# Attention and two dense blocks on one core: the first keys loaded in two parts with the constants behind them, and the end of each attention half reordered

## The chip, the cores and the metric

The kernel runs on one core of a Trainium2 chip. The metric is the device time of one execution in microseconds (us), read as the median of several executions. The core has five engines, each of which runs its own instructions in the order in which they stand: PE (matrix multiplication), DVE (vector), ACT (tables of functions, here tanh and exp), POOL and SP (the last issues most of the transfers). Transfers run on 16 DMA engines that all queues share.

## The reference

Three stages follow one another. All of it is float32, and the kernel keeps that accuracy on PE by splitting each operand into a high and a low part and adding three products.

```python
def _attn_ref(q, k, v, cap):          # 4 x 12 heads, 448 positions, 64 wide
    scale = 1.0 / np.sqrt(q.shape[-1])
    scores = scale * np.matmul(q, k.transpose(0, 1, 3, 2))
    scores = cap * np.tanh(scores / cap)
    scores = scores - np.max(scores, axis=-1, keepdims=True)
    attn = np.exp(scores)
    attn = attn / (np.sum(attn, axis=-1, keepdims=True) + 1e-09)
    return np.matmul(attn, v)
...
def _moe_ref(x, w_in, w_out):         # 1792 tokens, 768 -> 2048 -> 768
    h = x @ w_in
    return (h - np.tanh(h)) @ w_out
...
def _moe2_ref(x, w_in, w_out, g_ln):  # 768 -> 1024 -> 768
    h = x @ w_in
    sm = softmax(h)                   # over the row, with 1e-09 in the sum
    solu = h * sm
    ln = (solu - mean(solu)) / sqrt(var(solu) + 1e-06) * g_ln
    return ln @ w_out
```

## The kernel before, in words

The batch is cut into two halves, and each half runs attention, the first block and the second block in turn. Attention of a half takes 12 pairs of heads; a pair fills the 128 partitions (two heads of 64). The loop of `attention` runs over i from -4 to 13 and starts the steps of several pairs in each turn: `load` and `load_v` fetch q with the keys (tile kq, 512 columns of keys, then 448 of q) and v (vf), `split_qk` makes the high part kqh (L250) and the low part kql (L252) on DVE, `scores` does the score matmuls on PE (L274, L276) and tanh on ACT (L278), exp follows on ACT (L288), `values` multiplies with v on PE (L308) and carries the row sums of exp along as row 64 of its result, and `evict` (L318) copies that result and its sums into ou. Three small transfers then spread the sums over partitions for a cheap reciprocal: rs<-ou, `finish1` (reciprocal L327, rd<-rs at L329, and ou<-ou at L330, which brings the second head of the pair to partitions 64 to 127), and `finish2` (rb<-rd at L336, a broadcast of the reciprocals to all partitions). `finish3` multiplies (L355) and splits the result into xh (L356) and xl (L357), the operands of the first block.

The last pair, 11, goes another way: `finish_last` takes two reciprocals of one row of 448 (L345) and spreads each with a matmul over the selector sel (L346).

The first block's up projection on PE (hp, L403 and L405) begins with the pairs that are done, goes round its weights, and needs xh and xl of the pairs 8 to 11 last. Its nonlinear part on DVE (first instruction L437) and ACT follows each hp.

In the first half the weights arrive as 64-bit words (tile st, L101), are narrowed on DVE (L106 to L108, tile f), cast on ACT (L114) and their low part taken on DVE (L115; L168 for those that `early` spreads over attention as fetch, `high` and `low`). They are written to DRAM (d<-w, L131) so that the second half only reloads them (L186). Thirteen of these writes wait until the end of the first half's attention and stand together there in SP's queue (`while pending`).

The order on every engine inside attention is that of the code. The constants of the cap (capt and what is worked out of it: tscale, ncap, shift, guard, gcol; L75 to L86) stand at the start of the program.

Of the kernel before, what the change touches and what calls it, by code (L numbers as in the profile page):

```python
# [29 lines left out]
def fused_kernel(ctx, tc, qk_in, v, cap, w1, w2, w3, w4, gln, out):  # L30
# [15 lines left out]
    KW = qk_in.shape[3] - S  # L46

# [27 lines left out]
    nc.vector.reciprocal(tscale, capt)  # L75
    nc.vector.tensor_scalar_mul(tscale, tscale, 1.0 / math.sqrt(D))
    ncap = const.tile([P, 1], F32, name="ncap")
    nc.vector.scalar_tensor_tensor(ncap, capt, -1.0, capt, ALU.mult, ALU.min)
    shift = const.tile([P, 1], F32, name="shift")
    nc.vector.tensor_scalar(shift, ncap, 64.0, 0.0, ALU.add, ALU.min)  # L80
    guard = const.tile([P, 1], F32, name="guard")
    nc.vector.scalar_tensor_tensor(guard, ncap, math.log(1e-9), shift, ALU.add, ALU.add)
    nc.scalar.activation(guard, guard, AF.Exp)
    gcol = const.tile([P, 1], F32, name="gcol")
    nc.vector.memset(gcol, 0.0)
    nc.vector.tensor_copy(gcol[D:D + 1], guard[D:D + 1])  # L86
# [49 lines left out]
    def early():  # L136

        units = [(f"1_{c}_{half}_{i}", w1u[(c * 2 + half) * (NK // 2) + i])
                 for c in range(2) for half in range(2) for i in range(NK // 2)]
        units += [(f"2_0_{d}", w2u[d]) for d in range(NK)]  # L140
        units = units[:WA]
        stage = {}

        def fetch(k):
            key, src = units[k]
            if key in saved:
                w = wp.tile([P, 2, 512], F32R, tag="w", name="w")
                nc.gpsimd.dma_start(w.bitcast(F32), saved[key].bitcast(F32))
                ahead[key] = w
            else:  # L150
                stage[k] = words(src, nc.gpsimd)

        def high(k):
            key = units[k][0]
            if k in stage:
                w = wp.tile([P, 2, 512], F32R, tag="w", name="w")
                ahead[key] = w
                stage["f", k] = narrowed(stage.pop(k))

        def mid(k):  # L160
            if ("f", k) in stage:
                nc.scalar.copy(ahead[units[k][0]][:, 0], stage["f", k])

        def low(k):
            if ("f", k) in stage:
                key = units[k][0]
                w = ahead[key]
                nc.vector.tensor_tensor(w[:, 1], stage.pop(("f", k)), w[:, 0].bitcast(F32), ALU.subtract)  # L168
                pending.append((key, w))

        return fetch, high, mid, low
# [52 lines left out]
    def attention(ap, hb, xh, xl):  # L224
# [9 lines left out]
        def load(p):  # L234
            bb, j = pairs[p]
            kq = ap.tile([P, KW + S], F32, tag="kq", name="kq", bufs=3)
            with tc.high_priority(offset=400 if hb == 0 and p == 0 else 0):
                (nc.sync if hb == 0 and p < 3 else nc.gpsimd).dma_start(kq, qk_in[HB * hb + bb, j])
            raw[p] = kq

        def load_v(p):
            bb, j = pairs[p]
            vf = ap.tile([P, 8, VW], F32, tag="vf", name="vf", bufs=3)
            nc.gpsimd.dma_start(vf, v[HB * hb + bb, j])
            vs[p] = (vf,)

        def split_qk(p):
            kq = raw.pop(p)
            h = ap.tile([P, KW + S], F32R, tag="kqh", name="kqh")
            nc.vector.tensor_copy(h, kq)  # L250
            l = ap.tile([P, KW + S], F32R, tag="kql", name="kql")
            nc.vector.tensor_tensor(l, kq, h.bitcast(F32), ALU.subtract)  # L252
            qk[p] = (h, l)

# [8 lines left out]
        def score(p, r):  # L263
# [5 lines left out]
            cs = slice(P * r, P * (r + 1))  # L269
# [69 lines left out]
        def finish_last(p):  # L339

            ou, _ = fin[p]
            rec = ap.tile([P, 7, S], F32, tag="t", name="rec")
            rb = pst("rbp", "o")[:, 0, :S]
            for hh in range(2):
                nc.vector.reciprocal(rec[D:D + 1, hh], ou[D:D + 1, hh])  # L345
                nc.tensor.matmul(rb, sel[D:D + 1, hh], rec[D:D + 1, hh], start=(hh == 0), stop=(hh == 1))  # L346
            nc.sync.dma_start(ou[D:, 0], ou[:D, 1])
            fin[p] = (ou, rb)
# [14 lines left out]
        for i in range(-4, n + 2):  # L363
# [3 lines left out]
            at(i - 1, evict)  # L367
            if i == n:
                finish_last(n - 1)
            at(i - 2, finish2, m=n - 1)  # L370
# [12 lines left out]
            at(e - 3, low, m=WA)  # L383
            at(e - 1, high, m=WA)
            at(i - 4, finish3)
        finish3(n - 2)
        finish3(n - 1)
        while pending:
# [282 lines left out]
```

## Time and profile before

| | |
|---|---|
| median of 3 runs | 961.9 us (960.1, 961.9, 963.87) |
| the profiled execution | 963.42 us, its span 961.1 us |
| mean granted clock of TensorE in it | 0.996 |
| PE busy | 935.8 us (97%) |
| DVE, ACT, POOL busy | 612.0 us (64%), 420.6 us (44%), 50.1 us (5%) |
| moved by DMA | 145.65 MB, mean 152 GB/s |

A busy share is an average over stages. PE, at 97%, leaves some 25 us in which it does nothing, and the busy time also holds the stretch in which its clock was granted at half. The times below are counted from the start of the span.

### The profile page before, as it was taken

What the parts mean: (1) busy time and instruction counts of PE and PEld (TensorE: products, weight loads), DVE (VectorE), ACT (ScalarE), POOL (GpSimd) and SP (SyncE); (2) the same over time, 40 slices, a digit from 0 to 9 for tenths busy, and PEclk for the clock granted to TensorE, in tenths of its full rate; (3) what the DMA queues carried; (4) which work ended last, traced back from release to release, by engine and by line L of the source; (5) the groups of instructions that cost most, each with busy time, mean ns of one, the idle gap of its engine ahead of it and who ended that gap; (6) DMA issues with size and microseconds to landing.
All of it is one profiled execution on the core that took longest, in us unless ns stands there. A gap on an engine that the chain in (4) does not pass through costs nothing.

```text
span 961.1 us, 11645 instructions
## 1 busy us (share of the span) xinstructions
PE 935.8 (97%) x4512; PEld 751.5 (78%) x4512; DVE 612.0 (64%) x946; ACT 420.6 (44%) x502; POOL 50.1 (5%) x91
## 2 busy tenths in 40 slices
PE   6999989999998999999989999999999999999998
PEld 3444569998998898888855555799999999988887
DVE  4677777989989895588335665596064553405751
ACT  6878508645436122352147775085250331211321
POOL 2221000000000000001011110000000000000000
PEclk9999989999999999999999999999999999999999
DMA  6565483188585874442135642243232232312311
GB/s 243 175 173 163 129 314 138 52 295 310 201 296 188 294 267 172 158 171 89 50 140 181 198 155 72 94 150 107 91 121 107 102 110 88 110 41 91 127 50 49
DMA packets 48946, 145.65 MB, mean 152 GB/s; under 512 B 11708, under 2 KB 16188, under 8 KB 48892
## 3 DMA queue, kind: packets, MB, share of 16 engines
q1 hardware_dynamic: 41404, 114.57, 34.5%
q0 software_dynamic: 7344, 30.35, 9.8%
q8 instruction: 35, 0.57, 0.3%
q14 instruction: 19, 0.16, 0.1%
q10 hardware_dynamic: 144, 0.00, 0.0%
HBM read 98.73 MB, written 43.33 MB: 148 GB/s over the span
## 4 chain that ended last, share of the span: by engine, by line
PE 73%; DVE 15%; DMA 8%; ACT 2%; issue 2%; SPq 0%; DVEq 0%; ACTq 0%
PE hp L403 11%; PE o L308 10%; PE op L459 8%; PE hp L405 5%; PE s L274 5%; PE op L461 4%; PE hp L222 4%; PE hp L221 4%; PE hp L220 4%; PE oab L556 3%; PE oab L560 3%; PE oab L557 3%; DMA st<-in_moe_w_out_dram 2%; DVE f L107 2%; DVE f L108 2%; DMA st<-in_moe_w_in_dram 2%
## 5 line engine op out<-in xcount | busy, mean ns | idle before, releaser
L403 PE MATMUL hp<-xh,w 128*128 128x448 f32 x384 | 116.7, 372 | 7.7 <-DVE xh L356 4.8
L308 PE MATMUL o<-t,vf 128*65 128x448 f32 x288 | 116.9, 543 | 1.6 <-ACT t L288 1.4
L403 PE MATMUL hp<-xl,w 128*128 128x448 f32 x384 | 117.2, 371 | 0.4 <-DVE xl L357 0.4
L405 PE MATMUL hp<-xh,w 128*128 128x448 f32 x384 | 115.8, 368 | 0.0
L278 ACT ACTIVATE t<-s,tscale 128x896 f32<-128x896 f32 x96 | 82.3, 914 | 40.6 <-PE s L274 27.0
L459 PE MATMUL op<-gh,w 128*128 128x448 f32 x336 | 96.0, 367 | 0.5 <-DVE acc L468 0.5
L461 PE MATMUL op<-gh,w 128*128 128x448 f32 x336 | 96.2, 366 | 0.0
L459 PE MATMUL op<-gl,w 128*128 128x448 f32 x336 | 95.9, 366 | 0.0
L403 PEld LDWEIGHTS hp<-xh,w 128*128 128x128 f32 x384 | 72.3, 190 | 16.5 <-DVE xh L356 6.0
L308 PEld LDWEIGHTS o<-t,vf 128*65 128x65 f32 x288 | 37.6, 137 | 57.4 <-issue 47.1
L403 PEld LDWEIGHTS hp<-xl,w 128*128 128x128 f32 x384 | 72.8, 190 | 9.7 <-issue 1.7
L405 PEld LDWEIGHTS hp<-xh,w 128*128 128x128 f32 x384 | 72.6, 189 | 7.7 <-issue 1.5
L288 ACT ACTIVATE t<-t,shift,capt 128x1792 f32<-128x1792 f32 (+1 forms) x48 | 78.5, 1687 | 0.0
L468 DVE TENSOR_TENSOR acc<-op,acc 128x448 f32<-128x448 f32 x72 | 41.8, 617 | 44.0 <-PE op L461 44.0
L459 PEld LDWEIGHTS op<-gh,w 128*128 128x128 f32 x336 | 63.0, 188 | 6.4 <-issue 0.8
L459 PEld LDWEIGHTS op<-gl,w 128*128 128x128 f32 x336 | 63.1, 188 | 5.5
L461 PEld LDWEIGHTS op<-gh,w 128*128 128x128 f32 x336 | 63.1, 188 | 5.5
L222 PE MATMUL hp<-w,xl 128*128 128x512 f32 x168 | 65.5, 390 | 0.3 <-DVE xl L471 0.3
L220 PE MATMUL hp<-w,xh 128*128 128x512 f32 x168 | 65.6, 390 | 0.0
L221 PE MATMUL hp<-w,xh 128*128 128x512 f32 x168 | 65.4, 389 | 0.0
L431 ACT ACTIVATE u<-hp 128x896 f32<-128x896 f32 x32 | 29.5, 921 | 79.4 <-PE hp L405 79.3
L114 ACT CAST w<-f 128x512 fp32r<-128x512 f32 x44 | 27.4, 622 | 83.5 <-DVE f L108 56.9
(135 smaller groups left out, 1676.9 us busy)
## 6 DMA issues: line engine op xcount, KB each, us to landing
d<-w SPq DMA_DIRECT2D x69, 512.0 KB, 6.2
w<-d SPq DMA_DIRECT2D x56, 512.0 KB, 3.3
st<-in_moe_w_out_dram SPq DMA_DIRECT2D x35, 512.0 KB, 5.5
st<-in_moe_w_in_dram SPq DMA_DIRECT2D x24, 512.0 KB, 4.9
kq<-in_qk_dram POOLq DMA_DIRECT2D x21, 480.0 KB, 4.3
w<-d POOLq DMA_DIRECT2D x13, 512.0 KB, 5.5
vf<-in_v_dram POOLq DMA_DIRECT2D x24, 260.0 KB, 5.4
st<-in_moe_w_in_dram POOLq DMA_DIRECT2D x12, 512.0 KB, 6.2
```

Of the source, the lines that this page charges most:

```text
L220: nc.tensor.matmul(ps, sh, mh, start=first, stop=False)
L221: nc.tensor.matmul(ps, sh, ml, start=False, stop=False)
L222: nc.tensor.matmul(ps, sl_, mh, start=False, stop=last)
L274: nc.tensor.matmul(s[:, hh, :S], st[rows, cs], mv[rows, KW:], start=first, stop=last)
L278: nc.scalar.activation(t[:, 2 * r:2 * r + m], s[:, :m, :S], AF.Tanh, scale=tscale)
L288: nc.scalar.activation(t[:, sl], t[:, sl], AF.Exp, bias=shift, scale=capt)
L308: nc.tensor.matmul(o, vf[:, r + 5 * hh], t[:, 2 * r + hh], start=(r == 0), stop=False)
L403: nc.tensor.matmul(hp[:, g, :S], wh[:, ms], xs[g][i], start=(kk == 0 and i == 0), stop=False)
L405: nc.tensor.matmul(hp[:, g, :S], wl[:, ms], xs[g][0], start=False, stop=(kk == NK - 1))
L459: nc.tensor.matmul(op[:, g, :S], wh, gg[i][:, g], start=(m == 0 and i == 0), stop=False)
L461: nc.tensor.matmul(op[:, g, :S], wl, gg[0][:, g], start=False, stop=(m == nm - 1))
L468: nc.vector.tensor_tensor(a, op[:, g, :S], a, ALU.add)
```

## The change

The first part concerns the start. The host lays the key columns out in another order, so that the first 128 keys lie beside q. The first pair's kq is then fetched by two DMAs (576 columns, that is q and 128 keys; then 384 columns), `split_qk(0)` works in the same two parts, and the arithmetic of the cap is put behind it in a function `caps`. The first weight tile st and the first two vf are issued by SP instead of POOL. The second part concerns the end of attention, in both halves. `finish_last` spreads the raw sums with the two matmuls and takes one reciprocal of 128 x 448 from PSUM. `finish2` of pair 10 is put ahead of `finish_last`, the last four `finish3` run without other work between them, and the conversion of weights that stood between them follows behind.

```diff
@@ the constants @@
-    nc.vector.reciprocal(tscale, capt)
-    nc.vector.tensor_scalar_mul(tscale, tscale, 1.0 / math.sqrt(D))
...
+    def caps():
+        nc.vector.reciprocal(tscale, capt)
+        nc.vector.tensor_scalar_mul(tscale, tscale, 1.0 / math.sqrt(D))
+        nc.vector.scalar_tensor_tensor(ncap, capt, -1.0, capt, ALU.mult, ALU.min)
+        nc.vector.tensor_scalar(shift, ncap, 64.0, 0.0, ALU.add, ALU.min)
+        nc.vector.scalar_tensor_tensor(guard, ncap, math.log(1e-9), shift, ALU.add, ALU.add)
+        nc.scalar.activation(guard, guard, AF.Exp)
+        nc.vector.tensor_copy(gcol[D:D + 1], guard[D:D + 1])
...
-                stage[k] = words(src, nc.gpsimd)
+                stage[k] = words(src, nc.sync if k == 0 else nc.gpsimd)
...
-            with tc.high_priority(offset=400 if hb == 0 and p == 0 else 0):
-                (nc.sync if hb == 0 and p < 3 else nc.gpsimd).dma_start(kq, qk_in[HB * hb + bb, j])
+            src = qk_in[HB * hb + bb, j]
+            if hb == 0 and p == 0:
+                for cs in (slice(KQ0, KW + S), slice(0, KQ0)):
+                    nc.sync.dma_start(kq[:, cs], src[:, cs])
+            else:
+                (nc.sync if hb == 0 and p < 3 else nc.gpsimd).dma_start(kq, src)
...
-            nc.gpsimd.dma_start(vf, v[HB * hb + bb, j])
+            (nc.sync if hb == 0 and p < 2 else nc.gpsimd).dma_start(vf, v[HB * hb + bb, j])
...
+            for cs in (slice(KQ0, KW + S), slice(0, KQ0)) if hb == 0 and p == 0 else (slice(0, KW + S),):
+                nc.vector.tensor_copy(h[:, cs], kq[:, cs])
+                nc.vector.tensor_tensor(l[:, cs], kq[:, cs], h[:, cs].bitcast(F32), ALU.subtract)
             qk[p] = (h, l)
+            if hb == 0 and p == 0:
+                caps()
...
@@ finish_last @@
-            rec = ap.tile([P, 7, S], F32, tag="t", name="rec")
-            rb = pst("rbp", "o")[:, 0, :S]
+            rbp = pst("rbp", "o")[:, 0, :S]
             for hh in range(2):
-                nc.vector.reciprocal(rec[D:D + 1, hh], ou[D:D + 1, hh])
-                nc.tensor.matmul(rb, sel[D:D + 1, hh], rec[D:D + 1, hh], start=(hh == 0), stop=(hh == 1))
+                nc.tensor.matmul(rbp, sel[D:D + 1, hh], ou[D:D + 1, hh], start=(hh == 0), stop=(hh == 1))
             nc.sync.dma_start(ou[D:, 0], ou[:D, 1])
+            rb = ap.tile([P, S], F32, tag="rb", name="rb", bufs=3)
+            nc.vector.reciprocal(rb, rbp)
...
@@ the loop @@
+            at(i - 2, finish2, m=n - 1)
+            if i >= n:
+
+                at(i - 4, finish3)
             if i == n:
                 finish_last(n - 1)
-            at(i - 2, finish2, m=n - 1)
...
-            at(e - 3, low, m=WA)
-            at(e - 1, high, m=WA)
-            at(i - 4, finish3)
+            if i < n:
+                at(e - 3, low, m=WA)
+                at(e - 1, high, m=WA)
+                at(i - 4, finish3)
         finish3(n - 2)
         finish3(n - 1)
+        for i in (n, n + 1):
+            at(i + 2 - 3, low, m=WA)
+            at(i + 2 - 1, high, m=WA)
```

The lines of the changed kernel are numbered anew: what was L250 and L252 is L261 and L262, L75 to L86 became L83 to L89, L106 to L108 became L110 to L112, L115 became L119, L168 became L172, L355 to L357 became L367 to L369, L336 became L348, L347 became L357, and L437 became L456.

On DVE at the very start, behind the memsets, the kernel before has these rows (kqh and kql are the two parts of a pair's kq, the first two of them pair 0's):

```order
L75 RECIPROCAL tscale<-capt 128x1
L78 SCALAR_TENSOR_TENSOR ncap<-capt 128x1
L76 TENSOR_SCALAR tscale<-tscale 128x1
L80 TENSOR_SCALAR shift<-ncap 128x1
L82 SCALAR_TENSOR_TENSOR guard<-ncap,shift 128x1
L250 CAST kqh<-kq 128x960
L252 TENSOR_TENSOR kql<-kq,kqh 128x960
L86 COPY gcol<-guard 1x1
```

In the changed kernel DVE has at the same place:

```order
L261 CAST kqh<-kq 128x576
L262 TENSOR_TENSOR kql<-kq,kqh 128x576
L261 CAST kqh<-kq 128x384
L262 TENSOR_TENSOR kql<-kq,kqh 128x384
L83 RECIPROCAL tscale<-capt 128x1
L84 TENSOR_SCALAR tscale<-tscale 128x1
L85 SCALAR_TENSOR_TENSOR ncap<-capt 128x1
L86 TENSOR_SCALAR shift<-ncap 128x1
L87 SCALAR_TENSOR_TENSOR guard<-ncap,shift 128x1
L89 COPY gcol<-guard 1x1
```

The split of pair 0 moved ahead of the five small operations on the cap, and stands there in two parts.

On DVE at the end of the first half's attention, behind the eviction of pair 11, the kernel before has these rows (ou_836, ou_905, ou_943 and ou_972 belong to the pairs 8, 9, 10 and 11; w and f to weights):

```order
L345 RECIPROCAL rec_974<-ou_972 1x448 x2
L168 TENSOR_TENSOR w_931<-f_932,w_931 128x512
...
L357 TENSOR_TENSOR xl_109<-ou_905,xh_103 128x448
L355 TENSOR_TENSOR ou_943<-ou_943,rb_981 128x448
L115 TENSOR_TENSOR w_1565<-f_1568,w_1565 128x512
L356 CAST xh_104<-ou_943 128x448
L107 SCALAR_TENSOR_TENSOR f_1604<-st_1602,f_1604 128x512
L357 TENSOR_TENSOR xl_110<-ou_943,xh_104 128x448
L355 TENSOR_TENSOR ou_972<-ou_972,rbp_975 128x448
L108 SCALAR_TENSOR_TENSOR f_1604<-st_1602,f_1604 128x512
L356 CAST xh_105<-ou_972 128x448
```

In the changed kernel the same place reads (ou_839, ou_908, ou_946 and ou_975 are the pairs 8 to 11 here):

```order
L367 TENSOR_TENSOR ou_839<-ou_839,rb_912 128x448
...
L359 RECIPROCAL rb_986<-rbp_982 128x448
...
L367 TENSOR_TENSOR ou_946<-ou_946,rb_977 128x448
L368 CAST xh_97<-ou_946 128x448
L369 TENSOR_TENSOR xl_103<-ou_946,xh_97 128x448
L367 TENSOR_TENSOR ou_975<-ou_975,rb_986 128x448
L368 CAST xh_98<-ou_975 128x448
L369 TENSOR_TENSOR xl_104<-ou_975,xh_98 128x448
L172 TENSOR_TENSOR w_934<-f_935,w_934 128x512
L172 TENSOR_TENSOR w_963<-f_964,w_963 128x512
L119 TENSOR_TENSOR wx_1531<-f_1534,wx_1531 128x512
```

The three operations of pair 10 and of pair 11 now stand without another between them, the reciprocal is one instead of two, and fourteen rows of weight conversion (of L172, L119, L110, L111 and L112) stand behind them, ahead of the first row of the nonlinear part.

On SP at the same place the kernel before has (rd_969 and rb_981 are pair 10's, ou_972 pair 11's; d1_... are the weights written to DRAM):

```order
L329 DMA rd_969<-rs_945 112x8
L330 DMA ou_943<-ou_943 64x448
L347 DMA ou_972<-ou_972 64x448
L336 DMA rb_981<-rd_969 128x1x448
L131 DMA d1_0_0_0_998<-w_194 128x1024
```

In the changed kernel SP has:

```order
L341 DMA rd_972<-rs_948 112x8
L342 DMA ou_946<-ou_946 64x448
L348 DMA rb_977<-rd_972 128x1x448
L357 DMA ou_975<-ou_975 64x448
L135 DMA d1_0_0_0_1000<-w_197 128x1024
```

The copy of pair 11's second head moved from ahead of pair 10's broadcast to behind it. In the second half the reload of one weight (wx, 128x1024) stands between the two. The two matmuls of `finish_last` stand together on PE, soon behind the last `values`, and PE's order behind them is that of before.

## Rows read from the trace of the kernel before

**Rows 1.** The chain of work that ended last, its shares of the span.
```profile
PE 73%; DVE 15%; DMA 8%; ACT 2%; issue 2%; SPq 0%; DVEq 0%; ACTq 0%
```

**Rows 2.** Windows: length, then busy time (instructions) per engine, granted clock, DMA share, GB/s.
```profile
core 0: us, PE busy (x) PEld busy (x) DVE busy (x) ACT busy (x) POOL busy (x), PEclk, DMA share, GB/s
130.00:136.00 6.00, 1.88 (x7) 0.97 (x7) 2.91 (x8) 0.62 (x1) 0.00 (x0) 0.86 1.02 402
130.00:145.00 15.00, 10.86 (x38) 8.62 (x38) 8.70 (x18) 1.86 (x3) 0.00 (x0) 0.77 1.02 385
160.00:372.00 212.00, 208.63 (x1007) 188.23 (x1005) 197.44 (x300) 96.33 (x134) 1.60 (x3) 1.00 0.67 229
```

**Rows 3.** Timeline of the start: start, us, engine, line, operation, idle before and releaser.
```profile
6.21 0.16 DVE L75 RECIPROCAL tscale<-capt 128x1 f32<-128x1 f32 x1 [4.78 <-DMA capt<-in_cap_dram]
6.73 0.65 DVE L250 CAST kqh<-kq 128x960 fp32r<-128x960 f32 x1
6.85 0.20 ACT L83 ACTIVATE guard<-guard 128x1 f32<-128x1 f32 x1 [4.38 <-DVE guard L82]
7.42 1.16 DVE L252 TENSOR_TENSOR kql<-kq,kqh 128x960 fp32r<-128x960 f32 x1
9.79 3.59 ACT L278 ACTIVATE t<-s,tscale 128x896 f32<-128x896 f32 x4 [2.74 <-PE s L274]
15.20 1.72 PE L308 MATMUL o<-t,vf 128*65 128x448 f32 x4 [0.57 <-ACT t L288]
```

**Rows 4.** DMA queue of SP, 1.5 to 5 and 5 to 7 us: packets, MB, share.
```profile
q1 hardware_dynamic: 138, 0.50, 50.6%
q1 hardware_dynamic: 161, 0.53, 68.9%
```

**Rows 5.** Timeline of DVE and PE, end of the first half's attention.
```profile
119.54 5.76 DVE L345 RECIPROCAL rec<-ou 1x448 f32<-1x448 f32 x2
133.03 0.62 DVE L355 TENSOR_TENSOR ou<-ou,rb 128x448 f32<-128x448 f32 x1 [1.79 <-DMA rb<-rd]
134.95 0.69 DVE L115 TENSOR_TENSOR w<-f,w 128x512 fp32r<-128x512 f32 x1 [1.29 <-ACT w L114]
136.00 1.11 PE L403 MATMUL hp<-xh,w 128*128 128x448 f32 x2 [3.62 <-DVE xh L356]
```

**Rows 6.** Timeline of SP at the same place.
```profile
124.92 0.56 SPq L336 DMA_DIRECT2D rb<-rd  x1
125.53 14.35 SPq L131 DMA_DIRECT2D d<-w  x13
```

**Rows 7.** Windows behind the stall, and the next long wait of PE in the timeline.
```profile
136.00:141.31 5.31, 5.29 (x14) 4.27 (x15) 5.31 (x11) 1.24 (x2) 0.00 (x0) 0.51 1.02 407
141.31:147.20 5.89, 5.89 (x30) 5.38 (x29) 0.48 (x1) 0.00 (x0) 0.00 (x0) 1.00 0.95 306
292.87 0.64 PE L403 MATMUL hp<-xh,w 128*128 128x448 f32 x2 [2.32 <-DVE t L440]
```

**Rows 8.** Timeline, end of the second half's attention.
```profile
612.55 0.63 DVE L355 TENSOR_TENSOR ou<-ou,rb 128x448 f32<-128x448 f32 x1 [2.48 <-DMA rb<-rd]
613.66 0.47 PE L403 MATMUL hp<-xh,w 128*128 128x448 f32 x1 [0.91 <-DVE xh L356]
614.18 0.61 DVE L355 TENSOR_TENSOR ou<-ou,rbp 128x448 f32<-128x448 f32 x1
614.32 0.47 PE L403 MATMUL hp<-xl,w 128*128 128x448 f32 x1 [0.19 <-DVE xl L357]
```

**Rows 9.** Transfers of the tile ou, all of them: issue to landing.
```profile
DMA to landing us min/median/max: 2.4/6.8/9.4
```

**Rows 10.** Groups by line: engine, operation, out<-in, count | busy us, mean ns | idle before.
```profile
L115 DVE TENSOR_TENSOR w<-f,w 128x512 fp32r<-128x512 f32 x44 | 30.0, 684 | 2.1 <-ACT w L114 2.0
L106 DVE TENSOR_SCALAR f<-st 128x512 uint32<-128x512 uint32 x72 | 29.6, 422 | 13.1 <-DMA st<-in_moe_w_out_dram 7.0 <-DMA st<-in_moe_w_in_dram 6.0
L107 DVE SCALAR_TENSOR_TENSOR f<-st,f 128x512 uint32<-128x512 uint32 x72 | 49.1, 688 | 0.8
```

**Rows 11.** Timeline: DVE's first instruction of the nonlinear part, first half.
```profile
149.24 1.09 DVE L437 SCALAR_TENSOR_TENSOR gf<-u,hp 128x896 f32<-128x896 f32 x1 [7.45 <-ACT t L433]
```

More of the change, by code (lines that the diff above doesn't have):

```diff
@@ L46, in fused_kernel @@
     KW = qk_in.shape[3] - S
+    KQ0 = KW - 128
     NCHUNK = w2.shape[0] // NK
@@ L74, in fused_kernel @@
     tscale = const.tile([P, 1], F32, name="tscale")
-    nc.vector.reciprocal(tscale, capt)
-    nc.vector.tensor_scalar_mul(tscale, tscale, 1.0 / math.sqrt(D))
     ncap = const.tile([P, 1], F32, name="ncap")
-    nc.vector.scalar_tensor_tensor(ncap, capt, -1.0, capt, ALU.mult, ALU.min)
     shift = const.tile([P, 1], F32, name="shift")
-    nc.vector.tensor_scalar(shift, ncap, 64.0, 0.0, ALU.add, ALU.min)
     guard = const.tile([P, 1], F32, name="guard")
-    nc.vector.scalar_tensor_tensor(guard, ncap, math.log(1e-9), shift, ALU.add, ALU.add)
-    nc.scalar.activation(guard, guard, AF.Exp)
     gcol = const.tile([P, 1], F32, name="gcol")
     nc.vector.memset(gcol, 0.0)
-    nc.vector.tensor_copy(gcol[D:D + 1], guard[D:D + 1])
+    def caps():
[6 more added lines that the diff above has]
+        nc.vector.tensor_copy(gcol[D:D + 1], guard[D:D + 1])
     sel = const.tile([P, 2, P], F32, name="sel")
@@ L249, in split_qk @@
             h = ap.tile([P, KW + S], F32R, tag="kqh", name="kqh")
-            nc.vector.tensor_copy(h, kq)
             l = ap.tile([P, KW + S], F32R, tag="kql", name="kql")
-            nc.vector.tensor_tensor(l, kq, h.bitcast(F32), ALU.subtract)
+            for cs in (slice(KQ0, KW + S), slice(0, KQ0)) if hb == 0 and p == 0 else (slice(0, KW + S),):
+                nc.vector.tensor_copy(h[:, cs], kq[:, cs])
+                nc.vector.tensor_tensor(l[:, cs], kq[:, cs], h[:, cs].bitcast(F32), ALU.subtract)
             qk[p] = (h, l)
+            if hb == 0 and p == 0:
+                caps()
         def split_v(p):
@@ L268, in score @@
             s = pst("s", "s")
-            cs = slice(P * r, P * (r + 1))
+            cs = slice(KQ0 - P * r, KQ0 - P * r + P)
             for st, mv, first, last in ((h, h, True, False), (h, l, False, False), (l, h, False, True)):
@@ L627 @@
     both = _np.zeros((b, h // 2, 2, d, 512 + s), k.dtype)
-    both[..., :384] = kk[..., :384]
-    both[:, :, 0, :, 384:448] = kk[:, :, 0, :, 384:]
-    both[:, :, 1, :, 448:512] = kk[:, :, 1, :, 384:]
+    for r in range(3):
+        both[..., 384 - 128 * r:512 - 128 * r] = kk[..., 128 * r:128 * r + 128]
+    both[:, :, 0, :, 0:64] = kk[:, :, 0, :, 384:]
+    both[:, :, 1, :, 64:128] = kk[:, :, 1, :, 384:]
     both[..., 512:] = qq
```

## The prediction

> **What bounds the kernel now.** The chain of work that ended last comes first: PE holds 73% of it, DVE 15%, DMA 8% [rows 1]. PE is busy 97% of the span, so only a stretch in which PE stands still, or runs at the lower clock, can give time back. The windows show one such place [rows 2]: from 130 to 145 us PE is busy 10.86 of 15 with a granted clock of 0.77, and from 130 to 136 only 1.88 of 6. The other is the start, before the first matmul. From 160 to 372 PE is busy 208.63 of 212 and DVE 197.44, so that DVE has little room there.
>
> The timeline of the start shows what PE waits for [rows 3]. DVE waits for capt until 6.21, does the cap's five small operations, then the CAST of the whole kq from 6.73 (it waits for nothing, so kq had landed by then), then kql from 7.42. The first tanh starts at 9.79. From there ACT is what PE waits for: at 15.20, with the first `values`, it has waited 0.57 for exp. An earlier tanh is therefore worth its whole shift, until PE itself binds.
>
> Then the end of the first half's attention [rows 5]. DVE spends 119.54 to 125.3 on two reciprocals of one row, and goes into the `finish3` of pairs 8 and 9 late: of PE's 4.12 idle us from 130 to 136 [rows 2], 3.62 are the long wait for pair 10, and 0.50 lie before it. DVE has waited 1.79 us at 133.03 for pair 10's rb, which SP issued at 124.92 [rows 6]. Then L115 stands between pair 10's multiplication and its xh, and waits 1.29 for an ACT cast, so that PE gets xh only at 136.00, after 3.62 us of nothing. Behind that wait the clock is granted at 0.51, the lower level of 1.2 GHz: 13 matmuls begin in the 5.31 us before the one at 141.31 (14 in the row, with that at its edge), and afterwards one takes 0.20 (5.89 for 30) [rows 7]. A wait of 2.32 us at 292.87, on the other hand, passes without a word in the clock (1.00 in the window from 160 to 372 around it, [rows 2]). In the second half the same place costs .91 and .19 [rows 8], since pair 10's rb lands only at 612.5, and nothing stands between the three operations.
>
> **The change, part by part.** All times are of the profiled execution (963.42 us, 2.3 above its span), which is 1.5 longer than the median of the three; I take the difference that I work out here off the median.
>
> *Start.* The queue of SP moves 138 packets (0.50 MB) between 1.5 and 5 us and 161 in the next two [rows 4]. The 480 KB of kq(0) are 128 packets of 3840 bytes, so its last packet goes at about 4.9. The DMA share is only about half there, so I take it that the number of packets sets the pace, not their size. The first part of the split load (128 packets of 2304 bytes) then ends where the whole did, at 4.9, and the second part (128 more) at the pace of the next row at 4.9 + 128/80 = 6.5 to 6.6. From the last packet to landing the row of the CAST allows 0 to 1.8 us (6.73 - 4.9); I take 1.1 for the first part (6.0), and 0.7 for the second (7.3), where the engines are busier and its packets small. From the second landing DVE needs CAST 384/960 of 0.69 = 0.28, kql 384/960 of 1.16 = 0.46, the five cap operations 0.61 (6.21 to 6.82), and ACT's guard 0.20 with .03 before it: 1.6 us [rows 3]. Tanh starts at 8.9, gain **0.9**. Its other operands are earlier: the first score needs kql of the first part, 6.0 + 0.42 + 0.70 = 7.1, and PE then 1.2 as before (from the end of kql, 8.58, to 9.79): 8.3. Bounds: if bytes set the pace, both parts are there when capt is, and the five operations begin at about 6.9: tanh at 7.7, gain 2.1. If the second part lands at 8.4 (6.6 + 1.8), tanh is at 10.0, loss 0.2. One st and two vf are behind the three kq on SP now. PE asks for vf(0) in `values`, at 15.20 less what is gained, 14.3; at the pace of the second row (161 packets in 2 us) the three kq, the st and vf(0), 768 packets with kq(0)'s two parts, are through 8.0 us behind the first 128, at 12.9. I cost it at nothing, with 1.4 to spare; if it came later, PE would wait for it one for one. POOL loses three issues, which nothing waits for.
>
> The Trainium skill, "DMA: Bandwidth & Descriptors", Rules for kernel authors, speaks against this part: it wants many small transfers coalesced into one large one. Its section on the anatomy of one DMA gives a fixed 2.0 us to each (on POOL's path, where kq goes through SP); paid in full by the second part behind the first, it would put landing at 8.0 and tanh at 9.6, and the gain would be 0.2. No row here shows two transfers of one tile behind one another.
>
> *End, first half.* The reciprocal on DVE becomes one of 128 x 448 for two of 1 x 448 (5.76 for both); by its columns it takes 2.9, as one of them, so DVE saves 2.9. The two matmuls stand soon after `values` of pair 11 and wait for the eviction (done at 119.5); PE is there at about 119.6, so I cost that at nothing, and at up to 0.5 if the eviction is late. xh of pair 9 then comes before PE asks for it, and the 0.50 of waiting before the long one goes. Pair 10's rb is not moved: SP issues it when rd has landed, at 124.92, and it lands at 133.0 as before. Behind it the second half's rows show what three uninterrupted operations give [rows 8]: from L355's start (612.55) PE has xh after 1.11 and xl after 1.77. Applied to 133.03, PE has xh at 134.14 and xl at 134.80, where it had xh at 136.00. PE runs out at 131.9 instead of 132.4, so its wait is about 2.3 plus 0.25 for xl, instead of 3.62 + 0.5. Pair 11's xh (2.7 after 133.03, so 135.8) is asked for by the 19th matmul only, so it makes no wait.
>
> What that is worth hangs on the clock. *If it stays at full rate*, the 14th matmul starts at 134.80 + 11 x 0.20 = 137.0 instead of 141.31: gain 4.2. *If it falls as before*, until 141.17, PE does one in 0.37 from 134.14, 19 by then, where it had done 13: 6 x 0.20 = 1.2 gained, and up to 1.6 if the low stretch begins and ends .5 earlier as the wait does; I take **1.5**. The wait of 2.3 lies nearest to the row of 2.32 that cost no clock, but here a second wait stands right behind it and sums to 2.55; and the stretch at the lower clock was 13 matmuls before with 3.62. I take the fall as somewhat likelier.
>
> *Moved work.* Fourteen conversion rows now stand behind pair 11's on DVE: 2 of L168 (the same operation as L115), 3 of L115, 3 each of L106, L107 and L108 (as L107), together 5 x 0.684 + 3 x (0.42 + 0.69 + 0.69) = 8.8 us [rows 10]. DVE gets to them at 136.4 and is done at 145.2 at the latest. Its next row, L437, started at 149.24 and had waited 7.45 for ACT and PE [rows 11]; it would be asked for at 147.7 or, with the clock kept, at 145.0. So the move is hidden with 2.5 us to spare, or just so. If that cover goes, each us is one of DVE's, which is at 93% from 160 to 372.
>
> *SP's queue.* Pair 11's copy of its second head, issued at 122.51, now goes behind rb at about 125.5, ahead of the 13 writes d<-w. Copies of this tile land 2.4 to 9.4 us after issue [rows 9]: 127.9 to 134.9, and L355 of pair 11 asks for it at 134.7. Nothing to 0.2 on DVE, nothing on PE. *Second half:* rb is anchored as before, so .91 and .19 stay; the copy is behind a reload of 512 KB as well, and may land after 614.18, when L355 asks for it: 0 to 0.6, I take **0.2** of loss.
>
> **Sum.** 0.9 + 1.5 - 0.2 = 2.2: 963.42 would become 961.2, and the median 961.9 becomes **959.7**.
>
> **The rivals.**
> - *The clock stays* (0.25). 0.9 + 4.2 - 0.2 = 4.9: 957.0. For it the 2.32 us at 292.87, against it the second wait and that the clock had fallen in a wait at this very place.
> - *The gain at the end is taken back by DVE* (0.10). The moved conversions wait for ACT casts (L115 waited 1.29 at 134.95) and end after L437's turn, so the work from 149 on starts no earlier; only the start is left: 961.9 - 0.7 = 961.2. For it DVE's 93%, against it the 7.45 us of waiting before L437.
> - *The split load buys nothing* (0.12): the second part lands at 8.2 or later, by a price per transfer (the rule named above would do this). 959.7 + 0.9 = 960.6. For it that two transfers have twice the packets; against it the half-idle engines until 5 us.
> - *Slower* (0.08): pair 11's copy shares the 16 engines with 13 writes of 512 KB that follow it directly. 6.8 MB at 407 GB/s [rows 7] are 16.8 us: landing at 142.3 in the worst case. L355 and all that is queued behind it on DVE, the 14 conversions and L437, then stand: pair 11's xl is done at about 144.2, L437 starts at 152 to 153, 3.5 later than before; less the start, 961.9 + 3.5 - 0.7 = 964.7. It decides from a landing at about 138 on (138 + 1.9 + 8 reaches 147.7), 12.5 after the issue, where the longest seen is 9.4.
>
> **Numbers.** The forecast has 0.45. Its own range is 958.6 to 961 (start 0 to 2.1, end 1.2 to 2.0, second half -0.6 to 0). With the first three rivals the range is 956.2 to 961.6: it leaves out the slower case and the outer ends. 0.5% of 961.9 is 4.8 us, about what a measurement of this kernel can tell from no change. Faster by more than that is somewhat over half of the case in which the clock stays, and the forecast with the start's upper bound: 0.22. Slower by more than 4.8 is only the worst of the last rival: 0.05. The rest is 0.73.
>
> **What would show it.** Start: the first tanh at 8.9 instead of 9.79, and behind it everything up to the first hp earlier by as much; if DVE's second CAST of pair 0 starts after 8.2, the split step is wrong. End: DVE's three operations on pair 10 directly behind the landing of rb, PE's wait 2.3 instead of 3.62, and the granted clock in the window behind it, which decides between 1.5 and 4.2. DVE's wait before L437 should be 1 to 3 us; if it is none, the moved conversions bind. The forecast is wrong altogether if L367 of pair 11 waits for its copy, or if rb of pair 10 lands at another distance from its issue than 8 us.

## The result, and the profile after

The changed kernel takes 957.55 us (median of 20 runs), the kernel before 966.71 (median of 20). The ratio is 0.9903, with a 95% interval of 0.9882 to 0.9925: about 9 us, or 1%, are gained. One of the twenty runs of the changed kernel took 1160.05 us at a granted clock of 0.752, and the ratio is taken without it. The three runs that stood ahead of the prediction (median 961.9) were among the shorter of the twenty. So the forecast of 959.7 us lies near the measured time, inside its range, but the gain that it forecast, 2.2 us, is a quarter of the measured one. In the profiled executions the spans are 961.1 and 957.0, only 4.1 apart: the one of the kernel before (963.42 us) lay 3.3 below the median of its twenty, and the one of the changed kernel (959.22) 1.7 above.

The chain of work that ended last reads much as in [rows 1], with DVE's share up from 15% to 17%:

```profile
PE 72%; DVE 17%; DMA 7%; issue 2%; ACT 2%; SPq 0%; DVEq 0%; ACTq 0%
```

The start, in the timeline of the changed kernel (DVE, ACT and PE, columns as in [rows 3]):

```profile
5.14 0.46 DVE L261 CAST kqh<-kq 128x576 fp32r<-128x576 f32 x1 [3.71 <-DMA kq<-in_qk_dram]
6.31 0.35 DVE L261 CAST kqh<-kq 128x384 fp32r<-128x384 f32 x1
7.18 0.15 DVE L83 RECIPROCAL tscale<-capt 128x1 f32<-128x1 f32 x1
8.12 0.99 ACT L290 ACTIVATE t<-s,tscale 128x896 f32<-128x896 f32 x1
16.01 0.48 PE L288 MATMUL s<-kqh 128*128 128x448 f32 x1 [0.57 <-ACT t L290]
```

The first part of pair 0's kq has landed at 5.1 us, before capt is wanted at all. The second CAST runs at 6.31 without a wait, the cap's operations follow from 7.18, and tanh starts at 8.12 instead of 9.79. PE's last wait for ACT ends at 16.01; in the kernel before the same wait ended at 17.49:

```profile
17.49 0.47 PE L276 MATMUL s<-kqh 128*128 128x448 f32 x1 [0.57 <-ACT t L278]
```

So 1.5 us of the 1.7 stay. SP's DMA queue from 1.5 to 5 us and from 5 to 7 answers to [rows 4]:

```profile
q1 hardware_dynamic: 236, 0.44, 57.8%
q1 hardware_dynamic: 259, 0.79, 100.6%
```

236 packets instead of 138 went in the first stretch, with 0.44 MB instead of 0.50. DVE also uses the time until capt is there: before, it stood still for capt until 6.21 [rows 3]. No run has the cap behind a load in one part, so what the split and the order bring each is not shown.

The end of the first half's attention on DVE, and PE in the two windows of [rows 2] and [rows 7]:

```profile
119.97 2.96 DVE L359 RECIPROCAL rb<-rbp 128x448 f32<-128x448 f32 x1 [0.35 <-PE rbp L356]
133.37 0.63 DVE L367 TENSOR_TENSOR ou<-ou,rb 128x448 f32<-128x448 f32 x1 [8.58 <-DMA rb<-rd]
134.03 0.40 DVE L368 CAST xh<-ou 128x448 fp32r<-128x448 f32 x1
135.00 0.62 DVE L367 TENSOR_TENSOR ou<-ou,rb 128x448 f32<-128x448 f32 x1
```

```profile
130.00:136.00 6.00, 6.00 (x32) 5.55 (x30) 2.53 (x5) 0.00 (x0) 0.00 (x0) 1.00 1.02 400
136.00:141.31 5.31, 5.31 (x28) 4.93 (x27) 5.28 (x11) 0.86 (x2) 0.00 (x0) 1.00 1.02 406
```

DVE waits 8.58 us for pair 10's rb and gets it at 133.37, at about the time of before. PE does not wait for it at all: from 130 to 136 it is busy 6.00 of 6 us where it had been busy 1.88, and from 136 to 141.31 it starts 28 matmuls where it had started 14, at the full clock (1.00 instead of 0.51). This is the whole long wait and the whole stretch at the lower level. What is behind it is given back in part (ACT, DVE, then PE):

```profile
141.07 1.22 ACT L118 CAST w<-f 128x512 fp32r<-128x512 f32 x2 [3.67 <-DVE f L112]
142.20 0.92 ACT L450 ACTIVATE u<-hp 128x896 f32<-128x896 f32 x1
143.78 0.68 DVE L119 TENSOR_TENSOR w<-f,w 128x512 fp32r<-128x512 f32 x1
144.38 1.08 DVE L456 SCALAR_TENSOR_TENSOR gf<-u,hp 128x896 f32<-128x896 f32 x1
147.81 0.65 PE L422 MATMUL hp<-xh,w 128*128 128x448 f32 x2 [1.31 <-DVE t L459]
166.49 0.64 PE L422 MATMUL hp<-xh,w 128*128 128x448 f32 x2 [2.54 <-DVE t L459]
```

ACT stands for 3.67 us with two casts of weights, whose operand is one of the conversion rows that were moved on DVE (L112), and takes the first Square of the nonlinear part only at 142.20. DVE's first row of that part starts at 144.38, and PE then waits for DVE, 1.31 and 2.54 us.

PE's instructions in the first 150, 380, 640 and 830 us say where the lead goes. Of before:

```profile
0.00:150.00 150.00, 136.82 (x564) 76.34 (x565) 100.09 (x165) 91.67 (x93) 21.05 (x40) 0.98 0.63 205
0.00:380.00 380.00, 363.14 (x1651) 280.03 (x1652) 309.92 (x478) 199.00 (x240) 22.66 (x43) 0.99 0.64 216
0.00:640.00 640.00, 618.00 (x2904) 465.60 (x2905) 467.51 (x749) 327.26 (x381) 46.19 (x84) 0.99 0.54 180
0.00:830.00 830.00, 808.00 (x3841) 641.61 (x3842) 560.93 (x854) 391.99 (x462) 46.19 (x84) 1.00 0.49 164
```

and of the changed kernel:

```profile
0.00:150.00 150.00, 142.35 (x603) 83.01 (x604) 103.06 (x171) 96.69 (x100) 19.73 (x37) 1.00 0.64 202
0.00:380.00 380.00, 364.77 (x1678) 284.08 (x1679) 307.87 (x479) 199.51 (x241) 21.33 (x40) 1.00 0.65 216
0.00:640.00 640.00, 620.95 (x2941) 471.83 (x2942) 470.42 (x757) 333.19 (x388) 44.85 (x81) 1.00 0.55 182
0.00:830.00 830.00, 810.95 (x3860) 644.38 (x3861) 558.25 (x858) 392.88 (x464) 44.85 (x81) 1.00 0.50 164
```

The first number in brackets of a row is what counts: the matmuls that PE has started. The lead is 39 matmuls at 150 us (8 us at 0.2 each), 27 at 380, 37 at 640 and 19 at 830. Two things take from it: waits for DVE up to 380, and something in the second half's first block, from 640 to 830, where PE waits in neither kernel. There one matmul starts every 202.7 ns in the kernel before and every 206.7 ns in the changed one, as the counts below (x9) show. In two more executions of the changed kernel (below) the lead at 380 us is 41 and 32, so one pair of profiles fixes it only to some 10 matmuls, or 2 us.

### The profile page after: what moved, and what is told of

The parts are those of the page before. It is cut to its first block, busy times and chain, and to the rows that moved or that the text cites. A ratio compares the mean times of both kernels' runs of the same rounds, so it can differ in the third digit from the quotient of the medians.

```text
span 957.0 us, 11649 instructions
## 1 busy us (share of the span) xinstructions
PE 934.9 (98%) x4512; PEld 750.7 (78%) x4512; DVE 607.0 (63%) x946; ACT 420.4 (44%) x502; POOL 48.7 (5%) x88
## 4 chain that ended last, share of the span: by engine, by line
PE 72%; DVE 17%; DMA 7%; issue 2%; ACT 2%; SPq 0%; DVEq 0%; ACTq 0%
PE o L320 11%; PE hp L422 9%; PE op L478 8%; PE hp L424 5%; PE s L286 4%; PE op L480 4%; PE hp L226 4%; PE hp L225 4%; PE hp L224 4%; PE oab L575 3%; PE oab L579 3%; PE oab L576 3%; DMA st<-in_moe_w_in_dram 2%; DVE f L111 2%; DVE f L112 2%
## 5 line engine op out<-in xcount | busy, mean ns | idle before, releaser
L464 ACT CAST gh<-gf 128x896 fp32r<-128x896 f32 x32 | 30.0, 944 | 72.4 <-PE op L480 46.3
```

## The experiments

Ratios are to the kernel before on the same chip, of medians, with the 95% interval.

**The changed kernel again** (c0_again, c0_third), to see what differs between executions.

> The changed kernel itself once more, as a measure of what one execution differs from another. In the profiles at hand one matmul of the second half's first block took 206.7 ns from start to start (windows 640 to 800 us) in the changed kernel and 202.7 ns in the kernel before, which costs the changed kernel some 4 us from 630 to 830 us. Theory S: the pace is set by what the program does just before (before: PE waits .91 and .19 us at the start of that block; changed: no wait), so the pace here is 206.7 again. Theory C: it differs from execution to execution; then it may be 202.7 here. The time: 0.99 of before, within 0.3%.

> The changed kernel a third time, to set beside the one above: Square near 142 us with ACT's wait for the moved rows ahead of it, 0.990 to 0.992 against before. If the pace of the second half's first block goes by chance, it may be 202.7 ns here (it was 206.7 twice); if the program fixes it, 206.7 again.

Measured: 0.9915 (0.9883 to 0.9946) and 0.9892 (0.986 to 0.9924). The second half's first block went at 206.7 ns in both, and the ACT casts stood ahead of the first Square in both (the Square at 141.6 and 140.3 us).

**The start alone** (x1_start): the end of attention as before.

> The start alone (split load, cap behind it, one st and two vf on SP); the end of attention as before. Both theories of the end give the same here: the first tanh near 8.1 instead of 9.79 us, everything behind it 1.5 us earlier, PE's wait for pair 10 (3.62 us) and the stretch at the lower clock as before. Ratio 0.998 to 0.9985.

Measured: 0.9986 (0.9954 to 1.0018), no difference that can be told from none. The first tanh starts at 8.14. PE's two waits for pair 10, first and second half:

```profile
134.59 1.11 PE L415 MATMUL hp<-xh,w 128*128 128x448 f32 x2 [4.16 <-DVE xh L368]
611.48 0.74 PE L415 MATMUL hp<-xh,w 128*128 128x448 f32 x1 [3.17 <-DVE xh L368]
```

They are 4.16 and 3.17 us, where the kernel before had 3.62 and .91. In the first half rb is used 1.5 us earlier (131.56 instead of 133.03), so most of the start's 1.7 us passes this wait. In the second half it is used 2.2 us earlier (610.37 instead of 612.55); PE, which has started 2761 matmuls by 605 us where it had started 2743, is there by more than that and waits, and at 640 us nothing is left of the lead (2903 and 2904).

**The end alone** (x2_end): the start as before.

> The reordered end of attention alone (both halves), the start as before. Theory O (PE's order: the third hp's first half now stands ahead of the matmuls that need pair 10, so the wait is covered): no wait for pair 10, no fall of the clock, about 6.6 us gained at 150 us, 2 of them given back by 350 us to waits for DVE; ratio 0.992 to 0.995 against before. Theory P (the prediction's: only pair 10's shorter chain on DVE counts): a wait of 2 to 2.5 us stays and 1.3 to 4 us are gained; ratio 0.996 to 0.999.

Measured: 0.9942 (0.9908 to 0.9976), 5.6 us. PE has no wait for pair 10 in its profile. The two parts multiply to 0.9928, which agrees with the whole within the intervals.

**One copy added to the kernel before** (x4_free):

```diff
             nc.sync.dma_start(ou[D:, 0], ou[:D, 1])
-            fin[p] = (ou, rb)
+            rs2 = ap.tile([P, S], F32, tag="rb", name="rb", bufs=3)
+            nc.vector.tensor_copy(rs2, rb)
+            fin[p] = (ou, rs2)
```

> The kernel before with one copy added: the spread reciprocals of pair 11 go from PSUM to SBUF on DVE right behind the second matmul, so that the PSUM tile is free then; the two reciprocals, the order of the conversions on DVE and SP's order stay. In the built program the third hp's first 18 matmuls then stand ahead of those that need pair 10. Theory O: that is enough; the wait of 3.62 us and the lower clock go or shrink under 1 us, 3 to 6 us gained; ratio 0.994 to 0.997. Theory P: pair 10's chain on DVE is not shortened, so PE waits as before; ratio 0.999 to 1.002.

Measured: 0.9909 (0.9878 to 0.9941), as much as the whole change. The window of [rows 7] and PE's wait for pair 10:

```profile
136.00:141.31 5.31, 2.15 (x10) 1.39 (x8) 2.65 (x5) 0.62 (x1) 0.00 (x0) 1.00 1.03 410
140.34 0.48 PE L405 MATMUL hp<-xh,w 128*128 128x448 f32 x1 [2.66 <-DVE xh L358]
```

This fits neither expectation: the third hp stands ahead on PE, but the wait stays at 2.66 us (and the granted clock from 141.31 to 147.20 is 0.71), and the time is better than the one expected without it. The copy is not the only thing that differs. It takes one of the three buffers of rb ahead of pair 10's broadcast, and SP issues that broadcast when pair 8's multiplication has released another:

```profile
128.64 0.62 DVE L357 TENSOR_TENSOR ou<-ou,rb 128x448 f32<-128x448 f32 x1
129.28 0.56 SPq L336 DMA_DIRECT2D rb<-rd  x1
```

So pair 10's rb is used at 137.35, 4.3 us later than in the kernel before, and PE's wait is shorter even so: that is the order on PE, with a longer chain of pair 10. Most of this run's gain comes further behind, though:

```profile
0.00:150.00 150.00, 137.45 (x573) 78.01 (x574) 102.47 (x168) 93.60 (x96) 20.96 (x40) 0.99 0.61 195
0.00:380.00 380.00, 367.45 (x1679) 285.46 (x1680) 310.58 (x479) 200.03 (x241) 22.56 (x43) 1.00 0.65 216
```

The lead on the kernel before is 9 matmuls at 150 us and 28 at 380, since no wait for DVE of over 0.25 us follows here. Why none follows is not shown, and so the size of this run's gain does not measure what the covered wait is worth.

**PE's order of before in the changed kernel** (x5_order): the third hp is written behind the matmuls that need pair 10.

```diff
...
+            with tc.manual_schedule(engines={mybir.EngineType.PE}):
+                for m, g, k0, k1 in ((0, 1, 0, 3), (1, 1, 0, 3), (0, 1, 3, 4), (1, 1, 3, 4), (0, 1, 4, 5), (1, 1, 4, 5),
+                                     (2, 0, 0, NK), (2, 1, 0, 5)):
+                    up_mms(hps[m], wts[m // 2], m % 2, k0, k1, (g,))
...
```

> The changed kernel with PE's order behind the end of attention written out as the kernel before had it (the third hp behind the matmuls that need pair 10); DVE, SP and the start as changed. Theory O (PE's order covers the wait): PE stands still for pair 10 again, 2 to 4 us with the second wait, and the clock may fall; 600 matmuls are done 3 to 6 us later than in the changed kernel (149 us), of which the DVE-bound stretch behind takes up to 2 back; ratio to before 0.994 to 0.998. Theory P (pair 10's shorter chain on DVE is what counts): as the changed kernel, 0.991.

Measured: 0.9966 (0.9934 to 0.9998). This is the kernel that the prediction costed, with the start, DVE and SP as changed and PE as before:

```profile
133.16 0.74 PE L422 MATMUL hp<-xh,w 128*128 128x448 f32 x1 [3.59 <-DVE xh L368]
136.00:141.31 5.31, 5.31 (x22) 4.82 (x21) 5.31 (x11) 1.32 (x3) 0.00 (x0) 0.75 1.02 406
```

PE waits 3.59 us again, and the clock behind it is granted at 0.75 over the window. The difference to the changed kernel, some 6 us (0.9966 against 0.9892 to 0.9915, each give or take 0.003), is what PE's order is worth. The profiles show where it arises but not that it stays: x5_order has started 578 matmuls at 150 us where the changed kernel had 603, but 1674 at 380, against 1678, 1692 and 1683 in its three profiles.

**PE's order of the changed kernel in the kernel before** (x10_third): written by hand, the reciprocals in PSUM held as long as before.

> The kernel before, with PE's order written out by hand behind the end of attention: the third hp's first 18 matmuls ahead of the second halves of the first two, and the third taken along with them; nothing else changed, the PSUM tile of the spread reciprocals is held as long as before. The third hp lies in other PSUM banks (4 and 5) than that tile (6 and 7). Theory O in its narrow form (the order alone is the gain, and the early release only let the planner choose it): as the copy that frees the tile, 0.990 to 0.994, with PE's wait for pair 10 shrunk below 3 us or gone. Rival (the tile really has to be free on the chip): PE stands still ahead of the third hp until the multiplication of pair 11, and the ratio is 0.998 or more.

Measured: 0.9962 (0.9924 to 0.9999). The window of [rows 7], then DVE and PE behind it:

```profile
136.00:141.31 5.31, 5.31 (x28) 4.82 (x27) 4.45 (x9) 2.15 (x4) 0.00 (x0) 1.00 1.02 404
152.17 0.43 DVE L106 TENSOR_SCALAR f<-st 128x512 uint32<-128x512 uint32 x1 [9.41 <-DMA st<-in_moe_w_out_dram]
159.18 1.08 PE L403 MATMUL hp<-xh,w 128*128 128x448 f32 x2 [9.71 <-DVE t L444]
```

PE starts 28 matmuls in the window and waits for pair 10 nowhere: the order alone covers that wait, and the PSUM tile of the spread reciprocals need not be free for it. But the planner, which chooses the order on an engine where the code does not fix it, now put two weight conversions ahead of the first nonlinear row on DVE, DVE waited 9.41 us for their load, and PE 9.71 us for DVE. So of the expectation the part on the wait held and the part on the time did not; that the order is worth time rests on x5_order.

**The second half's end as before** (x6_hb1old), and **start and copy in one** (x7_both).

> The changed kernel with the second half's end of attention as in the kernel before; the first half's end and the start as changed. So far every kernel with the new end in the second half went through that half's first block at 206.7 ns a matmul (three profiles) and every one with the old end at 202.7 ns (three profiles). Theory S (the end sets the pace): 202.7 ns, 4 us less from 630 to 830 us, against a wait of 0.9 to 3.2 us for pair 10 that comes back; 0 to 3 us faster than the changed kernel, ratio 0.988 to 0.991. Rival (the pace goes with something else): 206.7 ns and 1 to 3 us slower than the changed kernel.

> The changed start, the old end, and the one copy that frees the PSUM tile early (the two kernels run before, in one). If what they gain adds up (0.9986 and 0.9909): 0.9895, that is 1.5 us less than the early release alone, and 202.7 ns a matmul in the second half's first block. If the earlier start only makes the waits for pair 10 longer (its sums go through two transfers that an earlier start does not make faster): 0.991, with waits of over 4 us at 135 us.

Measured: 0.9932 (0.9901 to 0.9963) and 0.9918 (0.9887 to 0.995). x6 went at 202.7 ns with waits of 1.11 and .19 for pair 10, and is not faster than the changed kernel. x7 is not better than the copy alone (0.9909); its wait for pair 10 was 2.68 at 138, not over 4. In it the copy delays pair 10's rb as in x4_free (issued at 127.03, when pair 8's multiplication from 126.38 is done). It went at 206.7 ns with the old end, so the end alone does not set the pace.

**One matmul more in the second half** (x9_extra).

> The changed kernel with one matmul more in the second half's end: the first of the two that spread the sums is done twice (about 0.8 us of PE). It tells whether the pace of the block behind hangs on how the instructions ahead of it fall, or on the absence of a wait. If the pace changes with so little: 202.7 ns, 3 us less than the changed kernel. If not: 206.7 ns and 0.8 us more.

Measured: 0.9913 (0.9881 to 0.9946). It began that block at 202.7 ns and fell to 206.7 at 637 us, without a wait of PE there, so it fits neither expectation. PE's counts from 700 to 750 us, in turn of before, changed, x4_free, x7_both, x8_between and x8_again:

```profile
700.00:750.00 50.00, 50.00 (x248) 46.36 (x247) 27.51 (x31) 14.91 (x17) 0.00 (x0) 1.00 0.34 120
```

```profile
700.00:750.00 50.00, 50.00 (x244) 45.41 (x243) 22.87 (x27) 11.30 (x13) 0.00 (x0) 1.00 0.30 99
```

```profile
700.00:750.00 50.00, 50.00 (x248) 46.41 (x247) 22.17 (x27) 12.24 (x15) 0.00 (x0) 1.00 0.29 95
```

```profile
700.00:750.00 50.00, 50.00 (x244) 45.41 (x243) 22.04 (x26) 11.23 (x13) 0.00 (x0) 1.00 0.29 95
```

```profile
700.00:750.00 50.00, 50.00 (x249) 46.34 (x248) 22.68 (x27) 12.09 (x14) 0.00 (x0) 1.00 0.35 109
```

```profile
700.00:750.00 50.00, 50.00 (x243) 45.42 (x243) 20.99 (x25) 12.87 (x15) 0.00 (x0) 1.00 0.29 95
```

248 or 249 instructions in 50 us are the pace of 202.7 ns, 243 or 244 that of 206.7. The last two rows are one program in two executions, with either pace. So the program alone does not fix the pace. That it is chance alone is not shown either: the four profiles with a wait for pair 10 in the second half (the kernel before, x1_start, x5_order, x6_hb1old) all went at 202.7 ns, and of the ten without one seven at 206.7, all three of the changed kernel among them. Whether the change makes the slower pace likelier stays open.

**The conversions back between the last steps** (x8_between, x8_again): the changed kernel without the move on DVE.

```diff
+            at(e - 3, low, m=WA)
+            at(e - 1, high, m=WA)
             if i < n:
-                at(e - 3, low, m=WA)
-                at(e - 1, high, m=WA)
                 at(i - 4, finish3)
         finish3(n - 2)
         finish3(n - 1)
-        for i in (n, n + 1):
-            at(i + 2 - 3, low, m=WA)
-            at(i + 2 - 1, high, m=WA)
```

> The changed kernel with the weight conversions back between the last steps of attention on DVE (they stand around the last finish3 as the planner puts them), ahead of what they stand behind in the changed kernel; reciprocal, SP and the start as changed. In the changed kernel the moved conversions end at 144.46 us and the first row of the nonlinear part starts at 144.38, 0.46 behind what it needs of ACT (143.92). If the move has a price: the first row starts up to 0.5 us earlier and PE's waits for DVE at 146 and 164 us (1.31 and 2.54) shrink as much; ratio 0.0005 better than the changed kernel. If pair 10's uninterrupted chain is worth something: its xh comes 1 to 2 us later, but PE, whose order still has the third hp ahead, does not ask for it; no difference. In both cases 0.990 to 0.992.

> The kernel with the conversions back between the last steps, once more, beside the changed kernel on the same chip. In its profile ACT took its casts of weights at 137.4 and 137.9 us and the first Square of the nonlinear part at 138.4, where in the changed kernel ACT waited 3.67 us for the moved DVE rows, cast at 141.07 and took that Square at 142.2. If that is the price of the move: the Square again near 138.5, DVE's first row of the nonlinear part near 141, PE's waits for DVE behind it together 2 to 4 us less than in the changed kernel, and a ratio to the changed kernel of 0.993 to 0.997 (0.984 to 0.988 against before). If the first result was the chance of the second half's pace (202.7 ns there): 0.991 against before.

Measured: 0.9837 (0.9798 to 0.9877) and 0.9857 (0.9825 to 0.9888); the medians of x8_again and of c0_third, on the same chip, are 955.58 and 958.25 (six runs each), a ratio of 0.997. ACT and DVE in x8_between, then ACT in x8_again:

```profile
137.36 0.62 ACT L118 CAST wx<-f 128x512 fp32r<-128x512 f32 x1 [2.75 <-DVE xl L369]
137.88 0.61 ACT L118 CAST w<-f 128x512 fp32r<-128x512 f32 x1
138.40 0.91 ACT L447 ACTIVATE u<-hp 128x896 f32<-128x896 f32 x1
141.01 1.08 DVE L453 SCALAR_TENSOR_TENSOR gf<-u,hp 128x896 f32<-128x896 f32 x1
```

```profile
136.97 0.62 ACT L118 CAST w<-f 128x512 fp32r<-128x512 f32 x1
137.88 0.92 ACT L447 ACTIVATE u<-hp 128x896 f32<-128x896 f32 x1 [0.30 <-PE hp L421]
```

The last cast starts at 137.88 and 136.97, and the first Square at 138.40 and 137.88, 2 to 4 us earlier than in the three profiles of the changed kernel (140.3 to 142.2). Part of that is when rb came: from pair 10's multiplication to the Square it is 6.1 and 6.5 us here (from 132.34 and 131.43) and 8.8 in all three profiles of the changed kernel (from 133.37, 132.78 and 131.45), so 2.4 to 2.8 us belong to the move. PE's counts agree: 702 and 707 matmuls started by 170 us where the changed kernel had 686, 681 and 688. The wait that cost this was not DVE's own behind the conversions (its first nonlinear row was late by 0.46 only) but ACT's, whose casts stand in order ahead of the Square. And the conversions had filled DVE's wait for rb: that wait is 1.79 us in the kernel before, 8.58 in the changed one, where they stand behind it, and 5.94 and 5.18 in these two runs. My expectation ahead of the first of these runs put the price at 0.5 us, since it looked at DVE's own lateness, and the second put it at 3 to 7.

## Why the prediction was right in sign and wrong in size

- **The step that failed** is PE's wait for pair 10, "about 2.3 plus 0.25 for xl, instead of 3.62 + 0.5", and under it the sentence ahead of the prediction that PE's order behind the two matmuls "is that of before". It is not, and PE waits nowhere for pair 10. Read with the buffer numbers, PE has in the kernel before, at the place in question (hp_1070 to hp_1072 are the first three hp; xh_104 and xl_110 hold pair 4 as their first tokens and pair 10 as their second, which these rows read):

```
L403 MATMUL hp_1070<-xh_104,w_313 128x448
L403 MATMUL hp_1071<-xh_104,w_313 128x448
L403 MATMUL hp_1070<-xl_110,w_313 128x448
L405 MATMUL hp_1070<-xh_104,w_313 128x448
L403 MATMUL hp_1071<-xl_110,w_313 128x448
L403 MATMUL hp_1072<-xh_100,w_381 128x448
```

and in the changed kernel (hp_1072 to hp_1074 are the first three there; these rows read first tokens), long before any row that needs pair 10 for its second tokens:

```
L422 MATMUL hp_1073<-xl_104,w_316 128x448
L424 MATMUL hp_1073<-xh_98,w_316 128x448
L422 MATMUL hp_1074<-xh_93,w_384 128x448
L422 MATMUL hp_1074<-xl_99,w_384 128x448
L424 MATMUL hp_1074<-xh_93,w_384 128x448
```

 Without the numbers the rows of three hp read alike, and the move cannot be seen. The planner that orders this block puts the third hp first once the PSUM tile of the spread reciprocals is read early (by the one reciprocal, or by the copy of x4_free). It takes 18 matmuls for the first tokens and 12 for the second ahead, 6.1 us at 0.2 each, so that PE asks for pair 10 after it is there. That x5_order, with the order of before, waits 3.59 us again, and that x10_third waits nowhere without the early reading, shows that the order is what removes the wait; why the planner waits for that tile, though the third hp lies in other banks, was not settled.
- **The sum under that assumption was near, as far as the interval tells.** x5_order has the assumed order, and its ratio, 0.9966 (0.9934 to 0.9998), is 3.3 us where I had 2.2. The wait it shows is 3.59 and not 2.3: PE runs out at 129.57, where I had 131.9, and xh comes at 133.16, where I had 134.14.
- **That the measured time lies in the range is in part luck.** The three runs ahead of the prediction had a median 4.8 us below that of the twenty; the gain forecast, taken off 966.71, would have given 964.5, 7 us too much. The one that stood nearest was the rival in which the clock stays, at 957.0, and its reason did not come about either: there was no wait behind which the clock could stay or fall.
- **The start** was mis-sized: 1.7 at tanh instead of 0.9. The two landings were at 5.1 and at 6.3 or before, instead of 6.0 and 7.3. 236 packets went where I had set the pace at 138; the smaller ones went faster. The cap's operations took 0.8 instead of 0.6. That the whole shift reaches PE was right for the first half's start (1.5 of 1.7). For the program x1_start cannot tell: its ratio allows 1.7 us as well as nothing, and its profile has lost the lead by 640 us. The rule of the Trainium skill, "DMA: Bandwidth & Descriptors", Rules for kernel authors, to coalesce many small transfers, shows no price here: the parts of 288 and 192 KB were in use from 5.14 and 6.31, where the row of the 480 KB shows them there by 6.73 [rows 3]. The fixed 2.0 us that the Trainium skill, "DMA: Bandwidth & Descriptors", gives in its section on the anatomy of one DMA, for POOL's path, would by the prediction's estimate have put tanh at 9.6, where the row has 8.12.
- **The clock** was what the prediction's two cases for the end hung on, the fall taken as somewhat likelier. It stayed at 1.00 in the window behind attention, where no wait came; so neither case is what happened. In x5_order, where a wait came, it was granted at 0.75.
- **The anchor held.** Pair 10's rb was used 7.9 to 8.1 us behind its issue in all fourteen profiles (125.38 and 133.37 in the changed kernel), where I had 8.
- **The moved work** was costed at nothing, with DVE's wait for ACT as its cover. DVE's backlog did end when I had it (144.46, where I had 145.2 at the latest), but its first nonlinear row follows at 144.38 without a wait, where I had set 1 to 3 us: by the prediction's own sign the moved conversions bind. What I left out is that DVE stands idle for rb ahead of them, and who waits for the moved rows: ACT's casts, in order ahead of the first Square. The price is 0.3% side by side (x8_again), and 0.6% to 0.8% by the ratio of x8_between.
- **The second half** was put at 0.2 of loss. Its waits of .91 and .19 went as well, for the same reason as in the first half. The profiled pair then loses 4 us to the slower pace; whether that belongs to the change stays open.
- **The slower rival** did not come: pair 11's multiplication ran at 135.00, directly behind pair 10's, and waited for no copy.

## What to carry to other kernels

Where a planner sets the order, look at the order of the engine that waits with every buffer's number on it; a shorter chain and a better covered chain both take from the same wait, and here the cover was worth more (some 6 of 9 us). Reading a tile early can change that order unasked, and a copy can take a buffer that another step needs, both as in x4_free. When work is moved out of a chain on one engine, ask whether it had filled a wait there, which in-order engine waits for its results, and what stands behind that wait. A kernel whose wait hangs on transfers that do not come earlier by as much gets little from starting earlier until that wait is covered.

## What the runs showed of the hardware that I had not expected

A row of equal matmuls (128x128 by 128x448) without any wait goes at one of two paces, 202.7 or 206.7 ns from start to start on the mean, at the same granted clock of 1.00, and can keep it for 190 us. It differs between two executions of one program (x8), and changed in x9_extra without a wait. Over the second half's first block this is 4 us, nearly half of the change. What sets it stays open. The clock's behaviour after waits of about the same length also differed: 2.54 us at 166 us cost nothing in the changed kernel, and 2.48 us at the same place was followed by 3.4 us at the lower level in c0_third:

```profile
166.00:170.00 4.00, 3.51 (x17) 3.30 (x18) 3.97 (x5) 3.86 (x5) 0.00 (x0) 1.00 0.00 0
```

```profile
164.60 0.64 PE L422 MATMUL hp<-xh,w 128*128 128x448 f32 x2 [2.48 <-DVE t L459]
165.42:168.82 3.40, 3.40 (x11) 2.99 (x10) 3.40 (x5) 2.67 (x4) 0.00 (x0) 0.50 0.00 0
```

Nor does a longer wait decide it: behind 3.21 us at 282 us in x8_again the granted clock is 1.00, and behind 2.24 us at 283 us in x8_between it is 0.59 from 284 to 288.
